# Low halves of the expert weights: all on VectorE instead of shared between VectorE and GpSimd

## The chip, the cores and the metric

One core of one Trainium2 chip runs the whole program. The metric is device time in microseconds (us), the median of three runs. Times inside the program are counted from the first profiled instruction of one profiled execution.

## The reference, cut to what matters

Three stages follow each other. Chunked attention makes 4608 token rows of 512 values. A mixture of eight experts sends each row to the expert with the largest gate logit and scales what comes back. A feed-forward part with a rational activation, P(h)/Q(h), makes the output.

```python
x = attention(q, k, v)                       # [4608, 512], chunks of 64 tokens, 8 heads
e = argmax(x @ w_gate)                       # one of 8 experts for each token
y = gate * (max(x @ w1[e], 0) @ w2[e])       # w1: [8, 512, 1024], w2: [8, 1024, 512], float32
h = y @ w_in                                 # float64 weights, [512, 2048]
out = (P(h) / (Q(h) + 1e-6)) @ w_out         # [2048, 512], float64
```

## The kernel before, in words

Every float32 matrix product of the experts and of the feed-forward part is made of three TensorE products: each operand is split into a high part (a copy rounded to the matmul type) and a low part (what the rounding left), and `mm3` (L257) adds high·high, high·low and low·high. The split of a weight tile is `split` (L132): ScalarE writes the high part (L136), and then one subtraction of a 128x1024 float32 tile writes the low part (L137). This subtraction reads two tiles in SBUF and writes a third. Its engine is the argument `eng`.

A weight tile goes through three steps. `fetch` (L208) takes one of four buffers of the pool `tmp` and has SP issue a 512 KB load. `split_w` (L139) takes a place in one of two rings of eight split tiles, and ScalarE and the engine `eng` fill it. The buffer is free for the load of the fourth tile after it once both have read it. Three callers choose the engine:

- In the attention loop, eight tiles of expert 0 are split at steps 16, 18, ... 30, all on GpSimd (L845).
- `weight()` (L228) splits the next tile of a list (`plan`) of 128 tiles for the expert stage: `w` tiles of each expert's fixed part of 512 tokens, `s` tiles for one further tile of 128 tokens, and the first half of the feed-forward weights. It is called after nearly every group of 12 products. Unless a caller names an engine, `alternate(c)` (L216) gives even tiles to VectorE and odd ones to GpSimd.
- `load_late` (L1267) splits the second half of the feed-forward weights on GpSimd, in 128x512 pieces, when the feed-forward part has begun.

What else VectorE does in the expert stage stands in the same order as in the code, because TensorE, VectorE and ScalarE keep the written order there (`manual_schedule` with MAN); GpSimd does not, and in the attention loop only TensorE keeps it, so a planner orders VectorE there. Beside the weights VectorE evacuates low parts of transposed rows (`to_T`, L255), low parts of the hidden layer (`relu`, L379) and results (L398), and in pieces rounds the float64 feed-forward weights to float32 (`convert`, L194, with `conv` at L167: L174 to L177, then L181 to L186). Most of these conversion steps read and write SBUF alone. In the attention part the chain of small operations that choose a token's expert (L681 to L690) lies on SBUF alone too. GpSimd's other work is the indirect transfers: the tokens' places (L788), gathers of rows (L237) and scatters of results (L243).

One expert of the loop `for e in range(1, NE)` takes 268 TensorE products and transposes. Within it the rows of the next expert are transposed in four steps `p(j)` into a PSUM tile of which there is only one (`ps_t`, bufs=1), so a `p(j)` has to wait until VectorE has written the low part of the one before it (L255).

Of the kernel before, what the change touches and what calls it, by code (L numbers as in the profile page):

```python
# [9 lines left out]
F32 = mybir.dt.float32  # L10
F32R = mybir.dt.float32r
BF16 = mybir.dt.bfloat16
I32 = mybir.dt.int32
U32 = mybir.dt.uint32
# [5 lines left out]
NT = 4608          # tokens  # L20
NTILE = NT // 128  # token tiles
NV = 3             # value tiles kept
NB = NT // 512     # blocks of the feed-forward part
NU = NTILE // 2    # units of two token tiles
NE = 8             # experts
BASE = 512         # slots of each expert's fixed part
LATE = 4           # the last units, whose tokens take no place among
X0 = NTILE - 2     # the step of the attention at which they do
EARLY = 384        # the first slots of expert 0: its tiles start while they are routed
NOVF = (NT - BASE) // 128   # most tiles that can lie beyond the fixed parts  # L30
NSTAT = 8          # tiles beyond the fixed parts that are unrolled
NOT_T = NT // 128  # tiles that an expert can have
PASSES = ((0, 0), (0, 1), (1, 0))   # hi*hi, hi*lo, lo*hi
CW = 256           # columns that are rounded to float32 at a time
# [3 lines left out]
EXP_BIAS = 893.0 * 2.0 ** 20   # float64's exponent bias less float32's, and 3, in place  # L38
# [3 lines left out]
def kernel(  # L42
# [19 lines left out]
    xs = dram.tile([NT, 512], F32, name="xs")               # attention's rows  # L62
    # experts' rows; behind them one row for each place that no token has
    ys = dram.tile([NT + NE * NT + NOVF * 128, 512], F32, name="ys")
    slots = dram.tile([NE * NT, 1], U32, name="slots")      # token of (expert, p, tile)
# [13 lines left out]
    # what the routing needs after the attention's end, and the other side of the SBUF  # L79
# [5 lines left out]
    # ---------------------------------------------------------------- constants  # L85
# [15 lines left out]
    rev = iota_f(once, "rev", [NE], [[-1, NE]], NE, 0)              # 8 - e  # L101
    rev2 = rev[:, None, :].to_broadcast([128, 2, NE])
    none = iota_f(once, "none", [1], [[0, 1]], NT, 1)               # row for the result of no token
# [5 lines left out]
    # the gate's weights, a quarter of the rows for each quarter of the PE array's columns,  # L109
    # and the sum of the quarters  # L110
# [7 lines left out]
    # coefficients of the rational function, P's negated  # L118
# [12 lines left out]
    # ---------------------------------------------------------------- weights  # L131
# [19 lines left out]
    # the feed-forward weights come as float64 words: rounded to float32 here  # L151
# [15 lines left out]
    def conv(job):  # L167
        raw, dst, m = job
        low, high = raw[:, :, 0], raw[:, :, 1]
        t = cv_p.tile([128, CW], I32, tag="cv", bufs=2, name=f"cv{m}")  # L170
        tf, lowf, highf = t.bitcast(F32), low.bitcast(F32), high.bitcast(F32)
        V = nc.vector
        # 2**(exponent - 3), with the sign
        V.tensor_scalar(t, high, 0x7ff00000, None, op0=ALU.bitwise_and)  # L174
        V.tensor_scalar(t, t, EXP_BIAS, EXP_BIAS, op0=ALU.max, op1=ALU.subtract)
        V.tensor_scalar(t, t, 3, None, op0=ALU.logical_shift_left)
        V.scalar_tensor_tensor(t, high, SIGN, t, op0=ALU.bitwise_and, op1=ALU.bitwise_or)  # L177

        def rest():
            # the upper 20 bits of the fraction, and the lower 32  # L180
            V.tensor_scalar(high, high, 0xfffff, 0x3f800000,  # L181
                            op0=ALU.bitwise_and, op1=ALU.bitwise_or)
            V.scalar_tensor_tensor(highf, highf, -0.875, tf, op0=ALU.add, op1=ALU.mult)
            V.scalar_tensor_tensor(lowf, low.bitcast(U32), 2.0 ** -55, tf,
                                   op0=ALU.mult, op1=ALU.mult)
            V.tensor_tensor(out=tf, in0=highf, in1=lowf, op=ALU.add)  # L186
            nc.sync.dma_start(dst, tf)

        return rest
# [4 lines left out]
    def convert(n):  # L194
        """n halves of the next jobs"""
        for _ in range(n):
            if half:
                half.pop()()
            elif fetched:
                half.append(conv(fetched.pop(0)))  # L200
            if jobs and len(fetched) + len(half) < 2:
                # behind the weights that are needed sooner
                with tc.issue_after(queued[-1]):
                    fetched.append(conv_fetch())
# [11 lines left out]
    def alternate(c):  # L216
        return nc.gpsimd if c % 2 else nc.vector

    # (source, buffers, list, place in it, name, order of the columns), in the order of use
# [14 lines left out]
    # ---------------------------------------------------------------- experts  # L234
# [14 lines left out]
    def to_T(src, hi, lo, nm, pool=None):  # L249
        # [128 rows, 512] -> four [128, 128] transposes, as hi and lo parts  # L250
        ps = (pool or ps_t).tile([128, 4, 128], F32, tag="h" if pool else "tp", name=nm)
        for c in range(4):
            nc.tensor.transpose(ps[:, c, :], src[:, 128 * c:128 * c + 128], ident)  # L253
        nc.scalar.activation(hi, ps, AF.Copy)
        nc.vector.tensor_tensor(out=lo, in0=ps, in1=hi.bitcast(F32), op=ALU.subtract)  # L255
# [50 lines left out]
    class Extra:  # L306
        """One tile of 128 tokens of any expert, in steps."""
# [51 lines left out]
    class Expert:  # L359
        """The fixed part of an expert's tokens, in steps."""  # L360
# [40 lines left out]
    # ---------------------------------------------------------------- attention  # L401
# [8 lines left out]
    # ---------------------------------------------------------------- feed-forward  # L410
# [22 lines left out]
    def first(b, c):  # L433
# [17 lines left out]
        if b == NB - 1 and c >= 12:  # L451
            # more of them at once, in the place of the next block's rows
            if c == 12:
                gts["last"] = xt_p[NB % 2].tile([128, 2, 4, 512], F32R, tag="xt", name="g_last")
            gt = gts["last"][:, :, c - 12]
        else:
            gt = h_p.tile([128, 2, 512], F32R, tag="h", name=f"g{b}_{c}")
# [26 lines left out]
    with man:  # L484
# [8 lines left out]
        for n in range(NV):  # L493
            # a pair of heads side by side: the second's columns are 0 in the first's rows,
            # the first's in the second's, so that one product takes both
            vt = v_p.tile([128, 2, 4, 2, 66], F32, name=f"v{n}")
            nc.gpsimd.memset(vt, 0.0)
            for j in range(2):
                nc.gpsimd.memset(vt[64 * j:64 * j + 64, :, :, j, 64:65], 1.0)
            vts.append(vt)  # L500
# [8 lines left out]
        def load_unit(u):  # L509
            nonlocal last_load  # L510
            r = [qk_p.tile([128, 8, 2, 64], F32, tag=nm, name=f"{nm}{u}") for nm in "qk"]
            # the first unit's in two halves, to start on the first of them
# [186 lines left out]
        # blocks' rows  # L699
        def load_rows(b):  # L700
# [6 lines left out]
            else:  # L707
                # in the place of the second block's transposed rows
# [33 lines left out]
        def early_counts():  # L742
            # what expert 0 has fewer than EARLY tokens by now
# [6 lines left out]
        def stage_rk(u):  # L750
            # ranks among the tokens of the same expert
# [14 lines left out]
            # the token's place: (expert, rank % 128, rank // 128)  # L766
# [36 lines left out]
        for i in range(NTILE + 1):  # L803
# [4 lines left out]
            if n == 0 and 0 <= g < 8:  # L808
                # expert 0's weights, behind the attention's own loads
# [33 lines left out]
            if n == 0 and 0 <= g < 8:  # L843
                with tc.issue_after(last_exp):
                    weights0[g] = split_w(raws0[g], "A", f"w0_{g}", g < 4, nc.gpsimd)  # L845
# [4 lines left out]
            # expert 0's first tiles, while the last tokens are routed  # L850
# [9 lines left out]
        # every expert's weights: of its fixed part in ring B, of its further tile in ring A  # L860
# [68 lines left out]
        # tokens of the experts' tiles  # L929
# [5 lines left out]
        # the rest of expert 0's fixed part  # L935
# [9 lines left out]
        # tiles beyond the fixed parts: (expert, tile) of the k-th one  # L945
# [59 lines left out]
        tab = const.tile([128, NOVF, 2], F32, name="tab")       # column, row if none  # L1005
        valid = small("valid", [NOVF])
        valid2 = small("valid2", [NOVF])
        etab = const.tile([128, NOVF], I32, name="etab")        # the expert
# [4 lines left out]
        pick(col, cbase)                                        # 32 e - cs  # L1013
# [15 lines left out]
        # gate probabilities  # L1029
# [10 lines left out]
        # the activation table that all that follows is in  # L1040
# [184 lines left out]
        # The first block's tokens rank below BASE among their experts' (a token's rank is at  # L1225
        # most its index), so their rows come from the fixed parts.
# [15 lines left out]
        # two products that run while the other engines come to the loop below  # L1242
# [4 lines left out]
        # the rest of the tiles beyond the fixed parts  # L1247
# [19 lines left out]
    def load_late(n):  # L1267
        # the second half's, in pieces that leave the other buffers alone
# [9 lines left out]
    # ---------------------------------------------------------------- feed-forward  # L1278
# [44 lines left out]
```

## Time and profile before

| | |
|---|---|
| three runs | 1591.93, 1591.75, 1588.03 us; median 1591.75 |
| profiled execution | span 1587.3 us; its own time beside the span is not among the times shown |
| busy in the span | TensorE 1485.4 us (94%), VectorE 1345.3 (85%), ScalarE 926.3 (58%), GpSimd 538.8 (34%) |
| GpSimd's subtractions that the change moves | 35 of `w` tiles, 87.7 us; 32 of `s` tiles, 82.5 us |
| mean granted TensorE clock | 0.974 |

The shares are means over stages with different limits. The attention part ends at about 225 us, the experts at about 745 us, and the rest is the feed-forward part. A row of a view names line, engine, operation, tiles written and read, shape and count; behind the bar stand busy time, mean ns of one instruction and the idle time before them with what ended it.

### The profile page before, as it was taken

How to read it: one execution, taken by the hardware profiler on the slowest of the kernel's cores; microseconds unless marked ns; L12 is line 12 of the kernel's file. 1: busy time of each engine (PE TensorE's matmuls, PEld its weight loads, DVE VectorE, ACT ScalarE, POOL GpSimd, SP SyncE). 2: the span in 40 equal slices, each digit the busy share in tenths (PEclk: the TensorE clock that was granted, in tenths of full speed). 3: DMA queues.
4: the chain of work that ended last, by engine and by line, in shares of the span. 5: the costliest groups of instructions: out<-in, count | busy, mean ns of one | idle time of the engine just before them, and what ended most of it. 6: DMA issues, size and time to landing. Idle time of an engine off the chain costs nothing.

```text
span 1587.3 us, 22356 instructions
## 1 busy us (share of the span) xinstructions
PE 1485.4 (94%) x7812; PEld 1213.4 (76%) x7812; DVE 1345.3 (85%) x2338; ACT 926.3 (58%) x1456; POOL 538.8 (34%) x374
## 2 busy tenths in 40 slices
PE   6888899998988989899889999999999999999998
PEld 5777777786867768677667888888888888888886
DVE  6788867799999999997788889888888888888886
ACT  5676644443434344344667666667676767676765
POOL 2123334544536355352453232322222222222222
PEclk9999999999989899999999999999999999999999
DMA  8999625676666676665220001010000101000000
GB/s 186 225 256 231 179 80 180 216 243 229 211 208 227 215 248 205 222 209 196 93 68 20 34 1 47 1 40 14 27 27 14 40 1 43 11 34 1 27 1 27
DMA packets 143377, 180.07 MB, mean 113 GB/s; under 512 B 51616, under 2 KB 96672, under 8 KB 143264
## 3 DMA queue, kind: packets, MB, share of 16 engines
q1 hardware_dynamic: 135712, 157.64, 33.0%
q0 software_dynamic: 7552, 21.00, 4.0%
q8 instruction: 62, 1.02, 0.3%
q14 instruction: 51, 0.42, 0.1%
HBM read 140.68 MB, written 37.91 MB: 113 GB/s over the span
## 4 chain that ended last, share of the span: by engine, by line
PE 45%; DVE 2%; issue 2%; POOL 1%; ACT 1%; DMA 0%; SPq 0%; ACTq 0%; POOLq 0%
PE z L259 23%; PE f L259 22%; PE ytp L253 1%; POOL g L459 1%; DVE t L449 1%; POOL wf L137 1%; DVE t L448 0%; DVE t L450 0%; DVE t L444 0%; DMA yg<-ys 0%; DVE t L446 0%; ACT u L445 0%; ACT t L440 0%; ACT t L441 0%; ACT u L442 0%
## 5 line engine op out<-in xcount | busy, mean ns | idle before, releaser
L259 PE MATMUL f<-yT,wf 128*128 128x512 f32 x1728 | 421.1, 395 | 5.7 <-DVE t L446 2.2
L259 PE MATMUL z<-wf,g 128*128 128x512 f32 x1680 | 411.1, 395 | 6.8 <-POOL g L459 4.1
L459 POOL TENSOR_TENSOR g<-t,g 128x512 fp32r<-128x512 f32 x140 | 209.5, 1498 | 531.8 <-ACT g L458 497.4
L259 PEld LDWEIGHTS f<-yT,wf 128*128 128x128 f32 x1728 | 324.7, 189 | 81.0 <-DVE t L446 3.1
L259 PEld LDWEIGHTS z<-wf,g 128*128 128x128 f32 x1680 | 314.7, 189 | 80.0 <-POOL g L459 5.9
L259 PE MATMUL y<-w,hT 128*128 128x512 f32 x744 | 195.7, 413 | 1.5 <-DVE hT L379 1.3
L443 DVE TENSOR_TENSOR t<-t,f 128x512 f32<-128x512 f32 x144 | 98.5, 684 | 100.7 <-ACT u L442 100.4
L259 PE MATMUL h<-xT,w 128*128 128x512 f32 (+1 forms) x768 | 182.0, 386 | 0.0
L259 PEld LDWEIGHTS y<-w,hT 128*128 128x128 f32 x744 | 144.6, 199 | 33.6 <-DVE hT L379 2.4
L259 PEld LDWEIGHTS h<-xT,w 128*128 128x128 f32 x768 | 142.3, 188 | 28.9 <-DVE hT L379 1.4
L444 DVE SCALAR_TENSOR_TENSOR t<-t,co,u 128x512 f32<-128x512 f32 x144 | 159.0, 1104 | 0.0
L445 ACT ACTIVATE u<-t,cq 128x512 f32<-128x512 f32 x144 | 104.6, 726 | 85.2 <-DVE t L444 84.7
L458 ACT ACTIVATE g<-t 128x512 fp32r<-128x512 f32 x140 | 89.0, 636 | 99.4 <-DVE t L450 99.3
L440 ACT ACTIVATE t<-f,co 128x512 f32<-128x512 f32 x144 | 112.0, 778 | 50.2 <-PE f L259 34.9
L137 POOL TENSOR_TENSOR w<-raw_w,w 128x1024 fp32r<-128x1024 f32 x35 | 87.7, 2506 | 120.9 <-ACT w L136 90.1
L450 DVE SCALAR_TENSOR_TENSOR t<-t,co 128x512 f32<-128x512 f32 x144 | 122.0, 847 | 2.0
L136 ACT ACTIVATE s<-raw_s 128x1024 fp32r<-128x1024 f32 x64 | 69.9, 1097 | 81.5 <-DMA raw_s<-in_moe_w_dram 81.5
L448 DVE SCALAR_TENSOR_TENSOR t<-t,u 128x512 f32<-128x512 f32 x144 | 101.7, 706 | 15.5 <-ACT u L447 15.5
L137 POOL TENSOR_TENSOR s<-raw_s,s 128x1024 fp32r<-128x1024 f32 x32 | 82.5, 2577 | 80.9 <-ACT s L136 80.7
L449 DVE SCALAR_TENSOR_TENSOR t<-t,u 128x512 f32<-128x512 f32 x144 | 109.5, 760 | 0.5
L442 ACT ACTIVATE u<-f,co 128x512 f32<-128x512 f32 x144 | 98.2, 682 | 15.0 <-DVE t L449 10.9
L446 DVE SCALAR_TENSOR_TENSOR t<-t,co,f 128x512 f32<-128x512 f32 x144 | 106.1, 737 | 0.0
(205 smaller groups left out, 2153.3 us busy)
## 6 DMA issues: line engine op xcount, KB each, us to landing
raw_w<-in_moe_w_dram SPq DMA_DIRECT2D x64, 512.0 KB
raw_s<-in_moe_w_dram SPq DMA_DIRECT2D x64, 512.0 KB
v<-in_v_dram SPq DMA_DIRECT2D x144, 64.0 KB
xs<-x SPq DMA_DIRECT2D x36, 256.0 KB
out_dram<-o SPq DMA_DIRECT2D x36, 256.0 KB
raw<-in_moe_w_in_dram SPq DMA_DIRECT2D x32, 256.0 KB
raw<-in_moe_w_out_dram SPq DMA_DIRECT2D x32, 256.0 KB
yg<-ys SPq DMA_DIRECT2D x32, 256.0 KB
```

The costliest lines, as they stand in the source:

```text
L137: eng.tensor_tensor(out=lo, in0=raw, in1=hi.bitcast(F32), op=ALU.subtract)
L259: nc.tensor.matmul(o, lhsT=lhs(x), rhs=rhs(y), start=(first and n == 0), stop=(last and n == 2))
L440: nc.scalar.activation(p, hp, AF.Identity, scale=a3, bias=a2)
L442: nc.scalar.activation(vv, hp, AF.Abs, scale=b0)
L443: V.tensor_tensor(out=p, in0=p, in1=hp, op=ALU.mult)
L444: V.scalar_tensor_tensor(qq, qq, b1, vv, op0=ALU.mult, op1=ALU.add)
L445: nc.scalar.activation(r, qq, AF.Abs_reciprocal_sqrt, bias=cq)
L446: V.scalar_tensor_tensor(p, p, a1, hp, op0=ALU.add, op1=ALU.mult)
L448: V.scalar_tensor_tensor(qq, qq, CQ, r, op0=ALU.add, op1=ALU.mult)
L449: V.scalar_tensor_tensor(qq, qq, -2.0, r, op0=ALU.add, op1=ALU.mult)
L450: V.scalar_tensor_tensor(p, p, a0, qq, op0=ALU.add, op1=ALU.mult)
L459: nc.gpsimd.tensor_tensor(out=gt[:, 1], in0=p, in1=gt[:, 0].bitcast(F32), op=ALU.subtract)
```

## The change

`alternate` returns VectorE for every tile, and the eight tiles of expert 0 that are split in the attention loop are given to VectorE. `load_late` keeps GpSimd. `load_extra`, which also calls `alternate`, is used in a loop that no tile of these inputs enters. Comments are taken out as well, with the line numbers kept.

```diff
     def alternate(c):
-        return nc.gpsimd if c % 2 else nc.vector
+        return nc.vector
...
             if n == 0 and 0 <= g < 8:
                 with tc.issue_after(last_exp):
-                    weights0[g] = split_w(raws0[g], "A", f"w0_{g}", g < 4, nc.gpsimd)
+                    weights0[g] = split_w(raws0[g], "A", f"w0_{g}", g < 4, nc.vector)
```

## Rows read from the trace of the kernel before

**Rows 1.** Page, part 2: VectorE's busy tenths and the granted TensorE clock, 40 slices.
```profile
DVE  6788867799999999997788889888888888888886
...
PEclk9999999999989899999999999999999999999999
```
**Rows 2.** Windows: stretch, length, busy us by engine, granted clock, DMA share, GB/s.
```profile
96.00:160.00 64.00, 51.82 (x603) 44.71 (x603) 54.17 (x168) 43.08 (x70) 23.57 (x17) 0.95 0.96 241
225.00:290.00 65.00, 61.53 (x316) 51.17 (x315) 41.25 (x91) 29.26 (x43) 29.46 (x20) 1.00 0.51 166
443.00:510.80 67.80, 61.28 (x269) 49.78 (x268) 64.92 (x110) 27.58 (x36) 31.47 (x18) 0.92 0.67 219
```
**Rows 3.** Waits, 290 to 745 us: total us, times, longest us.
```profile
ACT s L136 <- DMA raw_s<-in_moe_w_dram: 81.5, 31, 4.6
...
PE xtp L253 <- DVE xT L255: 35.9, 6, 6.9
```
**Rows 4.** Windows at TensorE's idle time, and behind it (sum of five such stretches).
```profile
443.00:449.90 6.90, 0.38 (x3) 0.03 (x1) 6.66 (x16) 2.18 (x3) 1.00 (x1) 0.69 0.84 286
...
382.20:387.60 5.40, 5.02 (x14) 4.15 (x15) 5.23 (x8) 2.90 (x4) 3.73 (x2) 0.51 0.97 367
...
sum 24.50, PE 23.84 PEld 19.69 DVE 22.03 ACT 12.90 POOL 16.17; mean PE 4.77 PEld 3.94 DVE 4.41 ACT 2.58 POOL 3.23
```
**Rows 5.** Timeline, VectorE and GpSimd, 490 to 496 us: start us, length us, instruction.
```profile
490.44 5.32 DVE L181 TENSOR_SCALAR raw<-raw 128x256 int32<-128x256 int32 x1
...
490.80 2.41 POOL L137 TENSOR_TENSOR w<-raw_w,w 128x1024 fp32r<-128x1024 f32 x1
...
493.15 2.45 POOL L137 TENSOR_TENSOR s<-raw_s,s 128x1024 fp32r<-128x1024 f32 x1
```
**Rows 6.** Single lines of the kernel: ns shortest/median/longest, first and last start.
```profile
L181 DVE TENSOR_SCALAR raw<-raw x64: 286/295/5344, 295.5 to 723.7; 128x256 int32<-128x256 int32 x64
...
L174 DVE TENSOR_SCALAR cv<-raw x64: 279/286/2536, 294.0 to 720.1; 128x256 int32<-128x256 int32 x64
```
**Rows 7.** Groups of VectorE's instructions, 290 to 745 us, by form.
```profile
L181 DVE TENSOR_SCALAR raw<-raw 128x256 int32<-128x256 int32 x64 | 65.3, 1020 | 1.3
L174 DVE TENSOR_SCALAR cv<-raw 128x256 int32<-128x256 int32 x64 | 45.6, 713 | 1.8 <-DMA raw<-in_moe_w_out_dram 1.8
...
L137 DVE TENSOR_TENSOR w<-raw_w,w 128x1024 fp32r<-128x1024 f32 x24 | 29.2, 1218 | 0.4 <-ACT w L136 0.2
...
L175 DVE TENSOR_SCALAR cv<-cv 128x256 int32<-128x256 int32 x64 | 27.6, 431 | 2.2
...
L176 DVE TENSOR_SCALAR cv<-cv 128x256 int32<-128x256 int32 x64 | 26.2, 409 | 2.2
```
**Rows 8.** Groups of GpSimd's instructions, 290 to 745 us.
```profile
L137 POOL TENSOR_TENSOR s<-raw_s,s 128x1024 fp32r<-128x1024 f32 x29 | 75.1, 2588 | 78.2 <-ACT s L136 78.0
L137 POOL TENSOR_TENSOR w<-raw_w,w 128x1024 fp32r<-128x1024 f32 x24 | 61.3, 2554 | 110.9 <-ACT w L136 81.3 <-DMA raw<-in_moe_w_out_dram 29.5
```
**Rows 9.** Waits, 96 to 233 us.
```profile
PE qkp L569 <- DVE kT L576: 17.5, 8, 2.7
```
**Rows 10.** Timeline, one unit of the attention loop, 122 to 128 us.
```profile
122.52 1.14 ACT L136 ACTIVATE w<-raw_w 128x1024 fp32r<-128x1024 f32 x1
...
123.74 2.40 POOL L137 TENSOR_TENSOR w<-raw_w,w 128x1024 fp32r<-128x1024 f32 x1 [0.66 <-ACT w L136]
...
123.89 2.29 DVE L684 TENSOR_TENSOR e<-lg_all,mx_all 128x16 f32<-128x16 f32 x1
...
126.83 0.69 DVE L576 COPY kT<-qkp 64x512 f32<-64x512 f32 x1
...
127.58 1.49 PE L569 MATMUL qkp<-ident,qkr 128*128 128x128 f32 x8 [2.71 <-DVE kT L576]
```
**Rows 11.** Groups of VectorE's instructions, 40 to 96 us.
```profile
L684 DVE TENSOR_TENSOR e<-lg_all,mx_all 128x16 f32<-128x16 f32 x6 | 1.0, 165 | 0.0
```
**Rows 12.** Timeline: load, high part and low part of one tile, 502 to 514 us.
```profile
502.14 1.22 DVE L137 TENSOR_TENSOR s<-raw_s,s 128x1024 fp32r<-128x1024 f32 x1
...
503.38 0.34 SPq L210 DMA_DIRECT2D raw_s<-in_moe_w_dram  x1
...
507.17 1.06 ACT L136 ACTIVATE s<-raw_s 128x1024 fp32r<-128x1024 f32 x1 [2.28 <-DMA raw_s<-in_moe_w_dram]
...
512.62 1.22 DVE L137 TENSOR_TENSOR s<-raw_s,s 128x1024 fp32r<-128x1024 f32 x1
```

## The prediction

> **What bounds the kernel now.** I read the page's slices first. VectorE is busy nine tenths or more from slice 9 to slice 18, which is the expert stage, and the granted clock of TensorE dips in the same part [rows 1]. The windows then separate the stages. One expert of the steady loop takes 67.8 us: VectorE is busy 64.9 of them, TensorE 61.3, at a mean clock of 0.92 [rows 2]. Between 225 and 290 us it is the other way, TensorE 61.5 of 65 and VectorE 41.3 [rows 2].
>
> The waits say how VectorE bounds the experts: TensorE waits there in one place, for the low part of a transposed tile from VectorE, 35.9 us in 6 waits, the longest 6.9 [rows 3]. That is one wait for each expert. In the window of such a wait VectorE is busy 6.66 of 6.9 us and TensorE 0.4; behind it TensorE works at a granted clock of about 0.5, the lower of its two levels (1.2 instead of 2.4 GHz), and five such stretches sum to 24.5 us [rows 4]. So VectorE is late, and TensorE pays for that twice.
>
> Why is VectorE late? The timeline shows one conversion step (L181) of 5.32 us. Two of GpSimd's subtractions, 2.41 and 2.45 us, lie inside it, one behind the other [rows 5]. The median of that instruction is 295 ns [rows 6]. An operation of VectorE on SBUF alone that comes while GpSimd subtracts ends only when GpSimd does. The instruction 5.32 us long is mostly a wait that the view counts as busy.
>
> **The change part by part.** 67 subtractions leave GpSimd: 8 in the attention loop, 53 (29 and 24) between 290 and 745 us [rows 8], and 6 between.
>
> *What VectorE gains in the expert stage.* I compare the mean with the median for the two conversion steps with both: L181 (1020 - 295) x 64 = 46.4 us, L174 (713 - 286) x 64 = 27.3 us. L175 and L176 are the same operation and shape; with 295 for each they lose (431 - 295) x 64 = 8.7 and (409 - 295) x 64 = 7.3 us [rows 6, 7]. That is 89.7 us, or 1.69 us for each of the 53 subtractions, a lower end because smaller groups are left out. The upper end is the pair seen directly, (5.32 - 0.30) / 2 = 2.5 us [rows 5]. I take 1.95, a little nearer the lower end, which sums over all instructions of these lines.
>
> *What VectorE pays.* Its own subtraction of such a tile takes 1218 ns [rows 7], against 2.55 to 2.59 us on GpSimd [rows 8]. Net VectorE gains 1.95 - 1.22 = 0.73 us for each moved tile. An expert has 8 of them, so 5.8 us (between 3.8 and 10).
>
> *What of it is on the path.* Of the six waits, the five large ones are about 6.7 us each. If VectorE comes 5.8 us earlier, 0.9 us stays in each: 35.9 - 5 x 0.9 = 31.4 us go. The 24.5 us at the lower clock held half the work, so 12.2 us come back if the clock no longer falls behind a wait this short. Together 43.6 us. The bounds: if all idle time goes it is 35.9 + 12.2 = 48.1; if VectorE sheds only 3.8 us, each wait stays near 2.9 us, which may be enough for the clock to fall, and 5 x 3.8 = 19 us are gained. What is late next is TensorE itself: 67.8 - 6.5 of idle - 2.4 of clock (a fifth of 12.2) leaves about 58.9 us of its own work for an expert, against 64.9 - 15.6 + 9.7 = 59.0 for VectorE. The two nearly meet, so I leave a rest of waiting.
>
> *The attention loop.* Eight times TensorE waits for VectorE's copy of k (L576), 17.5 us in total [rows 9]. The timeline of one unit shows why: GpSimd subtracts from 123.74 for 2.40 us; VectorE's tiny L684, begun at 123.89, takes 2.29 us; the copy of k comes at 126.83, and TensorE has idled 2.71 us [rows 10]. Undisturbed, L684 takes 165 ns [rows 11]. So 2.1 us are lost for each tile, and 1.22 takes their place if the subtraction stands ahead of the copy: 8 x 0.9 = 7 us gained, my value. If the planner puts it where VectorE has time, all 17.5 go, and some 6 us of lower clock that follow these waits by the windows' mean of 0.95 [rows 2]. If VectorE instead waits in line for ScalarE's high part (1.14 us [rows 10]), it is 8 x (1.22 + 1.14 - 2.1) = 2 us slower.
>
> *The six tiles between.* Between 225 and 290 us TensorE is the bound and VectorE has 24 us free [rows 2]; 6 x 1.22 = 7.3 us fit. I count nothing; without that cover it is 7.3 us.
>
> *Waits that are added.* VectorE now stands in line for the high part of every tile, and relu, transposed rows and conversions queue behind it, TensorE behind those. In the sample the load was issued at 503.38, the high part began at 507.17, and VectorE came to it only at 512.62, 4.4 us after the high part was written [rows 12]. That lead covers the wait. GpSimd's gathers and scatters no longer queue behind subtractions; nothing on TensorE's path waits for them, so nothing is counted. SP issues a load when its buffer is free, and only VectorE's progress releases it now: no new queue. The feed-forward part keeps its work.
>
> The Trainium skill, Perfetto Trace Analysis, section Optimizing Scalar/DVE Operations, speaks against the change: if DVE is saturated, some work may be given to ScalarE or even GpSimd. By that alone the moved work would come on top of the engine that bounds the experts. The same section adds that both share a read port, so that moving work between these two may not help. The conversion step of 5.32 us under two subtractions [rows 5] agrees with the addition.
>
> The sum: 43.6 + 7 = 50.6 us. Against the profiled span it is 1587.3 - 50.6 = 1536.7. The runs lie 0.7 to 4.6 us above that span (1588.03 to 1591.93), so the median becomes 1591.75 - 50.6, **about 1541 us**.
>
> **Rivals.**
>
> *More than that.* The attention's waits go as a whole. For it: units before 96 us have no such wait, and L684 is short there [rows 11]. Against it: DMA's share is 0.96 from 96 to 160 us [rows 2], so the loads would hold the loop soon. 43.6 + 17.5 + 6 = 67 us, 1525 us.
>
> *Half of it.* The stalls are at their lower end, the clock still falls and the attention gains nothing: 19 to 22 us, 1570 us. For it: VectorE and TensorE come within 1 us of each other in an expert, so each wait of VectorE for ScalarE counts.
>
> *Slower: VectorE waits for late tiles.* ScalarE waits 81.5 us for loads of `s` tiles, 31 times [rows 3]. All odd tiles of these were off VectorE's line. It decides when VectorE's work between one tile and the fourth after it becomes shorter than load, high part and low part: 3.8 + 1.06 + 1.22 = 6.1 us, against 512.62 - 503.36 = 9.3 us now [rows 12]. If all 81.5 us came on VectorE's path, 81.5 - 50.6 = 31 us would be lost: 1623 us. Against it: the 9.3 us hold two stalls (4 us less) and gain two subtractions (2.4 more), which leaves 7.7.
>
> *Slower: the stalls have another cause* and stay. Then VectorE has 67 x 1.22 = 82 us more where it is the bound: 1674 us. Against it stand the ends of instructions on both engines [rows 5, 10]. The rule of the Trainium skill's Perfetto Trace Analysis (Optimizing Scalar/DVE Operations) on a saturated VectorE would by itself give this time.
>
> **How the numbers follow.** Forecast 0.70, more 0.12, half 0.13, late tiles 0.03, other cause 0.02. The range: from 1520 (48.1 + 17.5 + 6 = 72 us gained) to 1570, the half case. About 0.3% is what a measurement of this kernel can tell from no change, 5 us. Faster holds the first two cases and most of the third, 0.92; same is what the half case leaves when late tiles eat the rest, 0.03; slower the last two, 0.05.
>
> **What would show it.** In the profile after: medians and means of L181, L174 and L684 nearly equal; no GpSimd subtraction before 745 us; TensorE's wait for L255 under 6 us in total and the clock at 1.00 through the experts; an expert's period near 59 to 60 us; the waits for L576 at about 10 us in total. It is wrong if VectorE's idle time before L137 grows to several us per expert, if the period stays above 64 us, or if the conversion steps stay long without GpSimd's subtractions.

## The result, and the profile after

The kernel after takes 1547.87 us (median of 4 runs, 1544.71 to 1549.44) against 1591.84 us before: a ratio of 0.9723, 95% interval 0.9705 to 0.9740, or 44 us. The forecast was 1541 us in a range of 1520 to 1570. The profiled execution took 1549.44 us with a span of 1547.7, 39.6 us shorter than the span before.

Where the 39.6 us lie can be read from two lines of the code. The last L684, near the end of the attention loop, starts at 229.7 us (229.1 before), and the first L440, at the start of the feed-forward part, at 717.7 (757.8 before). Between them 40.7 us are gone; the attention loop gave nothing here. (One profile cannot tell a few us in that loop: in another execution of the same kernel, E9 below, it ends at 221.0 us. The stretch between the two lines is 488.7 us there and 488.0 here.) The stretch as a whole, before and after (columns as in [rows 2]):

```profile
229.10:757.80 528.70, 484.68 (x2175) 393.57 (x2173) 475.75 (x810) 221.97 (x294) 234.89 (x139) 0.96 0.65 212
```

```profile
229.70:717.70 488.00, 474.41 (x2175) 385.92 (x2174) 420.23 (x869) 222.68 (x295) 91.87 (x80) 0.99 0.71 230
```

TensorE's idle time fell by 30.4 us, and its busy time for the same products by 10.3 us, at a higher clock. The page after (part 2, the rows that answer to [rows 1], and GpSimd's):

```profile
DVE  6787857799889898985989888888888888888886
...
POOL 2111122121211212102542222222222222222232
PEclk9999999999999999999999999999999999999999
```

In tenths TensorE's clock shows no dip in the experts' slices any more (two short ones are left, in the windows below), and VectorE is no longer full through all of them. The groups of VectorE, 290 to 710 us, answer to [rows 7]; the last two numbers ahead of the second bar are busy us and mean ns:

```profile
L137 DVE TENSOR_TENSOR w<-raw_w,w 128x1024 fp32r<-128x1024 f32 x48 | 58.5, 1219 | 0.0
...
L176 DVE TENSOR_SCALAR cv<-cv 128x256 int32<-128x256 int32 x64 | 19.6, 307 | 2.2
L175 DVE TENSOR_SCALAR cv<-cv 128x256 int32<-128x256 int32 x64 | 19.2, 300 | 2.2
L181 DVE TENSOR_SCALAR raw<-raw 128x256 int32<-128x256 int32 x64 | 18.5, 289 | 0.3
L174 DVE TENSOR_SCALAR cv<-raw 128x256 int32<-128x256 int32 x64 | 18.3, 286 | 0.0
```

The same 256 instructions shed 64 x (1020 - 289 + 713 - 286 + 431 - 300 + 409 - 307) ns = 89 us, and nothing in them was changed but GpSimd's company. VectorE's own subtraction of a `w` tile costs the 1219 ns that it cost before. The windows of three experts (columns as in [rows 2]):

```profile
407.00:469.10 62.10, 60.24 (x269) 48.72 (x269) 56.13 (x119) 27.25 (x37) 11.80 (x11) 0.97 0.74 242
469.10:530.30 61.20, 60.24 (x268) 48.73 (x268) 56.03 (x119) 26.32 (x36) 11.63 (x11) 0.97 0.76 244
530.30:592.50 62.20, 59.00 (x269) 47.49 (x269) 56.30 (x119) 28.60 (x38) 12.59 (x11) 1.00 0.78 241
```

An expert takes 62 us instead of 67.8, and VectorE is busy 56 us of them instead of 64.9. TensorE is busy 95 to 98 parts of a hundred: it is the bound now. What is left is in the waits, 290 to 710 us (to be set beside [rows 3]):

```profile
DVE yo L398 <- DMA ys<-yo,sidx: 17.0, 5, 4.1
ACT s L136 <- DMA raw_s<-in_moe_w_dram: 16.3, 20, 2.0
...
PE h L259 <- DVE hT L379: 6.4, 4, 1.8
...
PE xtp L253 <- DVE xT L255: 4.1, 6, 1.2
```

The wait for L255 fell from 35.9 us to 4.1. In its place stands a new one: VectorE waits up to 4.1 us for a scatter, and TensorE behind it up to 1.8 us. The timeline shows its place:

```profile
396.06 1.20 POOL L243 DMA_INDIRECT ys<-yo,sidx  x1 [0.30 <-issue]
...
397.86 0.98 POOL L243 DMA_INDIRECT ys<-yo,sidx  x1 [0.60 <-DVE cv L174]
...
403.10 0.69 DVE L398 COPY yo<-y 128x512 f32<-128x512 f32 x1 [4.12 <-DMA ys<-yo,sidx]
...
406.30 0.69 DVE L379 SCALAR_TENSOR_TENSOR hT<-h,hT 128x512 fp32r<-128x512 f32 x1
...
407.04 4.55 PE L259 MATMUL h<-xT,w 128*128 128x512 f32 x12 [1.83 <-DVE hT L379]
```

There are two buffers for output tiles (`o_p`). VectorE copies output tile 2 of the expert before into a buffer whose scatter was issued only a few us ago. By the semaphores of the trace it is the scatter issued at 396.06, of the tile that ScalarE had copied; it has landed at 403.00, and VectorE stood ready at 398.98. The low part L379 is queued behind that copy, and TensorE behind L379. In the kernel before VectorE came later, and the scatter had just landed:

```profile
478.49 1.06 POOL L243 DMA_INDIRECT ys<-yo,sidx  x1 [0.30 <-ACT yo L396]
...
483.96 0.69 DVE L398 COPY yo<-y 128x512 f32<-128x512 f32 x1 [0.55 <-ACT hTs L254]
```

There VectorE stood ready 4.9 us after the issue and the landing took 5.3 us; after, it is 2.9 and 6.9 us. Why the transfer takes longer is not shown.

### The profile page after: what moved, and what is told of

Read it like the earlier page. It is cut to its first block, busy times and chain, and to the rows that moved or that the text cites. A ratio compares the mean times of both kernels' runs of the same rounds, so it can differ in the third digit from the quotient of the medians.

```text
span 1547.7 us, 22303 instructions
## 1 busy us (share of the span) xinstructions
PE 1471.6 (95%) x7812; PEld 1198.5 (77%) x7812; DVE 1284.8 (83%) x2405; ACT 927.2 (60%) x1456; POOL 376.8 (24%) x307
## 4 chain that ended last, share of the span: by engine, by line
PE 46%; DVE 3%; issue 2%; POOL 1%; ACT 1%; DMA 0%; SPq 0%; ACTq 0%; POOLq 0%
PE z L259 23%; PE f L259 23%; PE ytp L253 1%; POOL g L459 1%; DVE t L449 1%; POOL wf L137 1%; DVE t L448 0%; DVE t L444 0%; DVE t L450 0%; DMA yg<-ys 0%; DVE t L446 0%; ACT u L445 0%; ACT t L440 0%; DVE yg L718 0%; DVE t L443 0%
## 5 line engine op out<-in xcount | busy, mean ns | idle before, releaser
L259 PE MATMUL y<-w,hT 128*128 128x512 f32 x744 | 184.0, 396 | 0.0
L259 PEld LDWEIGHTS y<-w,hT 128*128 128x128 f32 x744 | 136.9, 188 | 28.2 <-issue 0.4
L440 ACT ACTIVATE t<-f,co 128x512 f32<-128x512 f32 x144 | 112.1, 778 | 49.4 <-PE f L259 34.2
L378 ACT ACTIVATE hT<-h 128x512 fp32r<-128x512 f32 (+1 forms) x64 | 37.5, 585 | 147.0 <-PE h L259 114.1
L442 ACT ACTIVATE u<-f,co 128x512 f32<-128x512 f32 x144 | 98.3, 683 | 15.0 <-DVE t L449 10.9
L447 ACT ACTIVATE u<-u 128x512 f32<-128x512 f32 x144 | 90.4, 628 | 2.2
L441 ACT ACTIVATE t<-f 128x512 f32<-128x512 f32 x144 | 85.1, 591 | 0.0
```

The costliest lines, as they stand in the source:

```text
L259: nc.tensor.matmul(o, lhsT=lhs(x), rhs=rhs(y), start=(first and n == 0), stop=(last and n == 2))
L440: nc.scalar.activation(p, hp, AF.Identity, scale=a3, bias=a2)
L442: nc.scalar.activation(vv, hp, AF.Abs, scale=b0)
L447: last_act = nc.scalar.activation(r, r, AF.Square).ins
```

## The experiments

Ratios are to the kernel before, with 95% intervals. E1 to E4 were measured on one chip, E5 to E8 on a second, E9 to E12 on a third, each group beside the kernel before.

**E1: the attention loop alone.**

```diff
 # kernel before
-weights0[g] = split_w(raws0[g], "A", f"w0_{g}", g < 4, nc.gpsimd)
+weights0[g] = split_w(raws0[g], "A", f"w0_{g}", g < 4, nc.vector)
```

> The kernel before, with the eight tiles of the attention loop alone moved to VectorE. Theory of the prediction: 8 x (2.1 - 1.22) = 7 us faster than before, about 1585 us. Rival A: the loop gains nothing whoever subtracts (in the profile of the kernel after, its units take 11.8 to 11.9 us, as before), because the high part on ScalarE or the loads hold the loop: 1592 us, within 2 us of before. Units of 11.9 us either way would bear out the rival.

Measured: 1589.61 us, ratio 1.0025 (1.0008 to 1.0042). The seven microseconds of the prediction are not there; the kernel is even 4 us slower by the median. Where it loses them is not shown: in E1's profile the loop ends at 222.0 us, earlier than in the kernel before, and loop ends scatter by more than this. TensorE's waits, 96 to 233 us, of the kernel after show what became of the 17.5 us of [rows 9]:

```profile
PE xtp L652 <- DVE x L642: 5.1, 4, 1.8
PE xtp L652 <- ACT qkr L550: 4.7, 4, 1.2
...
PE ru_all L671 <- ACT lt L665: 4.2, 1, 4.2
...
PE qkp L569 <- ACT xt L656: 4.0, 8, 1.2
...
PE qkp L569 <- issue: 2.8, 6, 0.6
```

The wait for the copy of k has gone, and five smaller ones sum to 20.8 us. L684 has no stall left in this kernel (median 167 ns, longest 176), so the stall itself did go.

**E2: the experts alone.** The kernel after, with that one line back on GpSimd.

```diff
 # kernel after
-weights0[g] = split_w(raws0[g], "A", f"w0_{g}", g < 4, nc.vector)
+weights0[g] = split_w(raws0[g], "A", f"w0_{g}", g < 4, nc.gpsimd)
```

> The kernel after, with the eight tiles of the attention loop given back to GpSimd. If the whole gain comes from the 59 later tiles: 1548 us, within 3 us of the kernel after. If the attention loop gave 7 us of the 44: 1555 us.

Measured: ratio 0.9719 (0.9684 to 0.9753), against 0.9723 for the whole change. The other 59 tiles bring all of the gain.

**E3: half of the odd tiles back on GpSimd.**

```diff
 # kernel after
     def alternate(c):
-        return nc.vector
+        return nc.gpsimd if c % 4 == 3 else nc.vector
```

> The kernel after, with every fourth tile (the last of each four, half of the 59) back on GpSimd. Theory: each GpSimd subtraction stalls VectorE by about 2 us, so the conversion steps keep about half of their excess (the mean of L181 near 600 to 700 ns, between 289 and 1020) and the time is about half way: 1560 to 1575 us. Rival (VectorE has spare time now and takes any mix): within 3 us of 1548. Rival (two engines share the work best): below 1545 us.

Measured: 1589.93 us, ratio 1.0026 (1.0008 to 1.0044). Half of the moved work undone takes away all of the gain, which no theory had expected. The mean of L181 was forecast at 600 to 700 ns and is 395: the stalls fell on other instructions as well. E3's timeline shows why; lines of both engines:

```profile
425.83 6.23 DVE L137 TENSOR_TENSOR s<-raw_s,s 128x1024 fp32r<-128x1024 f32 x1
...
426.19 2.40 POOL L137 TENSOR_TENSOR w<-raw_w,w 128x1024 fp32r<-128x1024 f32 x1
...
428.54 2.43 POOL L137 TENSOR_TENSOR s<-raw_s,s 128x1024 fp32r<-128x1024 f32 x1
...
442.45 2.43 DVE L181 TENSOR_SCALAR raw<-raw 128x256 int32<-128x256 int32 x1
...
447.39 1.12 PE L253 MATMUL xtp<-ident,xg 128*128 128x128 f32 x4 [8.07 <-DVE xT L255]
```

A subtraction on VectorE of 1.2 us takes 6.23, because two of GpSimd's run back to back inside it. The Trainium skill, SBUF — State Buffer, section Who interferes with whom, says that a VectorE instruction with two SBUF inputs contends with a GpSimd instruction that reads SBUF, and that the issue order decides who blocks. The rows agree on the contention, and they add that VectorE did not get in between two GpSimd instructions in a row. On the order they do not decide: by the records the VectorE instruction began first (425.83 against 426.19), and it is the one that waited. A further stall of 2.1 us follows at 442 us. Together 7.2 us lie in the last 22 us before TensorE's wait for the transposed rows ends (447.39), and that wait is 8.07 us long, longer than any in the kernel before [rows 3]. In the same stretch VectorE also waits 1.75 us for a load of float64 weights (11.2 us in 5 such waits from 290 to 745 us; the kernel after has none), so the stalls are not the whole of it. The waits of E3 in sum, 290 to 745 us:

```profile
PE xtp L253 <- DVE xT L255: 42.8, 6, 8.6
DVE yo L398 <- DMA ys<-yo,sidx: 18.1, 6, 4.0
```

What VectorE saves earlier in the expert it loses in the wait for the scatter. So not the sum of the stalls but their place seemed to count. E10 tests that.

**E4: every tile of the list on GpSimd that no caller gives to VectorE.**

```diff
 # kernel after
     def alternate(c):
-        return nc.vector
+        return nc.gpsimd
```

> All tiles of the expert list on GpSimd that the callers do not pin to VectorE (even ones too); attention tiles on VectorE. VectorE then does 8 subtractions fewer per expert than in the kernel before (9.8 us less of its own work) and 16 fewer than after. Theory of the stall: 16 GpSimd subtractions an expert, each stalling VectorE by about 2 us: 64.9 - 9.8 + 8 x 1.95 = 70.7 us an expert against 67.8, so slower than before by 15 to 40 us, 1607 to 1632. Rival (the long conversion steps have another cause, and VectorE's own work sets the pace): VectorE sheds 59 us over the stage and the kernel is as fast as after or faster, 1545 to 1550. GpSimd itself has room: 16 x 2.55 + 10 = 51 us of an expert.

Measured: 1688.42 us, ratio 1.0645 (1.0591 to 1.0699). VectorE has less work of its own than in any other kernel here, and the time is the longest: the rival that sees only VectorE's own work is out. The direction is the theory's, the size is not (102 us against 15 to 40). Groups and waits, 290 to 745 us:

```profile
L181 DVE TENSOR_SCALAR raw<-raw 128x256 int32<-128x256 int32 x55 | 59.7, 1085 | 1.3
L176 DVE TENSOR_SCALAR cv<-cv 128x256 int32<-128x256 int32 x55 | 55.8, 1015 | 1.9
```

```profile
ACT s L136 <- DMA raw_s<-in_moe_w_dram: 113.8, 26, 12.1
...
PE xtp L253 <- DVE xT L255: 60.7, 10, 7.5
PE h L259 <- DVE hT L379: 29.9, 8, 9.6
...
DVE cv L174 <- DMA raw<-in_moe_w_out_dram: 19.5, 9, 3.6
DVE cv L174 <- DMA raw<-in_moe_w_in_dram: 17.1, 10, 3.4
```

There are more stalls, TensorE waits in two places, and ScalarE and VectorE wait longer for loads. That these start late because buffers come free late is argued from the code. From the last L684 to the first L440 (221.3 to 855.3 us) VectorE is busy 527.0 us against 475.8 before, 51 us more; the theory's 5.8 us for each of eight experts make 46. The stretch grew by 105 us, so about half of the loss is time in which VectorE waits, and that half the theory did not have. No wait of TensorE for GpSimd's own low parts is listed.

**E5 and E11: the copy of output tile 2 later.**

```diff
 # kernel after, in the loop over experts
                 cur.first(0)
-                old.out(2)
                 weight()
                 convert(1)
                 cur.relu(0)
                 late.t(1)
+                old.out(2)
                 cur.first(1)
```

> The kernel after, with the copy of output tile 2 of the expert before put behind the hidden layer's low part and one transposed tile, instead of ahead of them. In the kernel after VectorE waits 4.1 us there for the scatter of an earlier output tile (17.0 us, 5 times), and TensorE then waits 1.8 us for the low part (6.4 us in all) and runs 3.4 us at the lower clock twice. Theory (this is the wait that took the place of the old one): the wait for the low part goes, 6.4 + 3.4 = 10 us faster than after, about 1537 us, an expert near 59 us instead of 62. Rival (the wait for the scatter only moves, and VectorE is late for the next thing): within 3 us of after.

Measured: ratio 0.9692 (0.9671 to 0.9713). Its waits, 290 to 710 us:

```profile
DVE w L137 <- ACT w L136: 11.2, 7, 4.1
...
PE xtp L253 <- DVE xT L255: 8.0, 9, 3.2
...
DVE yo L398 <- DMA ys<-yo,sidx: 0.6, 2, 0.4
```

The wait for the scatter is gone (17.0 to 0.6 us), and no wait of TensorE for L379 is listed any more; 8.0 us at L255 remain. The gain is a few us, so it was measured again beside the kernel after on one chip, as E11 with E9:

> The kernel with the copy of output tile 2 later, once more beside after on one chip: 3 to 9 us faster than after (the stage of the experts was 5 us shorter in the profile).

> The kernel after once more, on the same chip as the next three, as their common measure: 0.972 of before, 1545 to 1551 us where before runs at 1592.

Measured on one chip: kernel after (E9) 1545.15 us, 0.9743 (0.9725 to 0.9762); copy later (E11) 1537.85 us, 0.9699 (0.9680 to 0.9717). It is 7 us faster (10 were forecast for E5), and the new wait is shown to have cost about that. An expert of E11 takes 60 us:

```profile
484.20:544.10 59.90, 58.67 (x268) 47.58 (x268) 56.44 (x119) 27.82 (x36) 11.80 (x10) 1.00 0.78 248
```

**E6, E7, E8: what holds the attention loop.** Each was timed once, so only the length of the loop's units is read. A unit is the time from one L684 to the next, here the mean of five units between about 125 and 186 us.

```diff
 # E6, kernel after: the high part stands in for the low part of expert 0
-weights0[g] = split_w(raws0[g], "A", f"w0_{g}", g < 4, nc.vector)
+nc.scalar.activation(hi, raw, AF.Copy)
+weights0[g] = w[:, 0:1].to_broadcast([128, 2, 1024])
 # E7, kernel after: one load, split eight times
-raws0[g] = fetch((w1r if g < 4 else w2r)[0, g % 4], f"w0_{g}")
+raws0[g] = raws0[0] if g else fetch(w1r[0, 0], "w0_0")
 # E8, kernel after: one tile, loaded and split once, in the place of all eight
+weights0[g] = weights0[0] or split_w(raws0[0], "A", "w0_0", True, nc.vector)
```

> The kernel after, without the eight subtractions of expert 0 in the attention loop: the products take the high part in the low part's place, so expert 0's low parts are left out. Loads and high parts stay. If the subtraction is what holds the loop's units at 11.8 us, they fall to 9.5 to 10.5 us and the loop ends 8 to 18 us sooner; if the high part on ScalarE or the loads hold them, they stay at 11.5 us or more.

> The kernel after, with one load for expert 0: all eight tiles are split from the same 512 KB, so seven loads (3.6 MB) are left out, and high and low parts are written eight times as after. If the loads hold the loop (DMA share 0.91 to 0.96 from 40 to 160 us), the units fall below 11 us; if not, they stay at 11.8 us and the DMA share falls.

> The kernel after, with one tile for all eight of expert 0: seven loads, high parts and subtractions are left out of the attention loop. If the tiles are what lengthens the units from about 9.5 us (before 96 us) to 11.8, they stay near 9.5 us, and the loop ends some 15 us sooner. If they stay at 11 us or more, the loop is held by its own chain of operations, and neither engine's subtraction could have gained there.

Measured: E6 11.1 us, E7 11.9, E8 9.4, against 11.9 in the kernel after and 12.2 before. But E1, whose engines have the same order in this loop as in the kernel after, has 11.2, and E2, with the order of before, 11.5. E10 has 12.1 with the order of after, E12 10.9 with the order of before. So two executions of the same loop differ by up to 1.3 us, and E6 cannot be told from a kernel with the subtraction. Loads are not it: DMA's share from 96 to 160 us fell from 0.91 to 0.80 in E7 and the units stayed. The tiles as a whole are it: without seven of them (E8) the units, 9.4 us, lie below that spread, and the loop ends at 216.1 us, ahead of every other kernel. Ends of the loop (last start of L684) in E1 and E8:

```profile
L684 DVE TENSOR_TENSOR e<-lg_all,mx_all x18: 164/165/176, 40.6 to 222.0; 128x16 f32<-128x16 f32 x18
```

```profile
L684 DVE TENSOR_TENSOR e<-lg_all,mx_all x18: 165/166/176, 40.8 to 216.1; 128x16 f32<-128x16 f32 x18
```

What remains beside the subtraction is the high part on ScalarE, 1.1 us in each unit. It was not taken out alone, so whether it or the subtraction holds the loop stays open.

**E10: 14 tiles on GpSimd, early in each expert.** The kernel after, with one constant more, so its lines stand one further down.

```diff
+ODD = {f"w1_{e}_{c}" for e in range(1, 8) for c in (1, 3)}
...
-                        eng or alternate(c if type(c) is int else c[1]))
+                        nc.gpsimd if nm in ODD else nc.vector)
```

> The kernel after, with 14 tiles back on GpSimd: the second and fourth w1 tile of each expert from 1 to 7, which are split early in an expert, ahead of the place where VectorE then waits 4.1 us for the scatter of an output tile. Theory after the run with half of the odd tiles: it is not the sum of the stalls that counts but where they lie, and only those between that wait and TensorE's wait for the transposed rows (some 40 us later) are paid. Then these 14 cost nothing: within 4 us of after in the same call. Rival (the sum of the stalls counts): 14 x (2.1 - 1.22) = 12 us slower than after.

Measured: 1542.39 us, 0.9730 (0.9707 to 0.9753), against 0.9743 for the kernel after on the same chip: no loss. The stalls are there (timeline of both engines):

```profile
391.02 3.01 POOL L138 TENSOR_TENSOR w<-raw_w,w 128x1024 fp32r<-128x1024 f32 x1 [3.20 <-ACT w L137]
...
391.65 2.53 DVE L175 TENSOR_SCALAR cv<-raw 128x256 int32<-128x256 int32 x1
```

But they fall into time that VectorE would have waited. First the waits of E9, the kernel after on the same chip, then those of E10, both 290 to 710 us:

```profile
DVE yo L398 <- DMA ys<-yo,sidx: 19.9, 6, 4.2
...
PE h L259 <- DVE hT L379: 7.0, 4, 1.9
```

```profile
PE xtp L254 <- DVE xT L256: 9.4, 10, 2.3
...
DVE yo L399 <- DMA ys<-yo,sidx: 0.8, 3, 0.4
```

VectorE's 19.9 us of waiting for the scatter are 0.8 here. 14 GpSimd subtractions in one place cost nothing, half of the odd ones (29) spread over the list (E3) cost all 44 us. The counts differ, so this alone would not tell place from sum. VectorE's busy time (third column of engines) from the last L684 to the first L440 does, in E9, E10 and E3:

```profile
221.00:709.70 488.70, 473.15 (x2176) 384.70 (x2174) 420.40 (x870) 222.98 (x295) 93.52 (x80) 1.00 0.72 229
```

```profile
226.10:710.90 484.80, 470.91 (x2175) 383.47 (x2173) 433.71 (x855) 222.72 (x295) 122.40 (x94) 1.00 0.72 231
```

```profile
224.70:762.60 537.90, 481.64 (x2176) 392.53 (x2174) 452.53 (x840) 221.37 (x295) 159.71 (x109) 0.96 0.65 208
```

E10 is busy 13.3 us more than E9 and no slower. E3 is busy 23.2 us less than the kernel before (475.75) and no faster, while 18.1 us of VectorE's waiting for the scatter stay unused. That is the place, not the sum. A run with as many tiles late in each expert was not made.

**E12: copy later, attention loop on GpSimd.** E5 with E2's line.

> The copy later and the eight tiles of the attention loop on GpSimd as in the kernel before. If where those eight are split is worth nothing: within 4 us of the kernel with the copy later. If the loop with VectorE is the slower one (the run of the attention part alone was 1.0025 of before): 2 to 6 us faster, the best of all.

Measured: 1535.91 us, 0.9683 (0.9664 to 0.9703). It is within 2 us of E11, whose interval it overlaps, and 9 us faster than the kernel after: the best version here beats both kernels.

## Why the prediction was right, point by point

- *VectorE bounds the experts, blocked by GpSimd.* Right. The four lines of the conversion are short again, E4 lengthens them and the time, and VectorE's own work cannot explain either.
- *1.95 us stall for a tile, 1.22 us paid.* Somewhat too low. The four lines alone shed 89 us, the lower end of 1.69 us by 53. With all lines VectorE's busy time fell by 55.5 us (475.75 to 420.23) for 59 tiles, 0.94 us net for each where 0.73 was forecast; for an expert by 8.8 us (64.9 to 56.1), where 5.8 was forecast within 3.8 to 10.
- *Which part of it is on the path.* Right for this change, but not as a rule. I priced every stall of an expert alike. E3 and E10 show that a stall is paid only where VectorE has no wait behind it that takes it up before TensorE waits. In the kernel before VectorE hardly waited (busy 64.9 of 67.8 us, and no wait of it for a scatter is listed), so nearly every stall was paid.
- *0.9 us of waiting left in each expert.* The wait for L255 is 4.1 us in 6, forecast 4.5; that is luck, because with 8.8 us shed the same subtraction (6.7 - 8.8) leaves none. The wait that came instead was put at nothing: of gathers and scatters the prediction says that nothing on TensorE's path waits for them. VectorE did wait for the scatter, through the two output buffers, and TensorE behind it. That costs 6.4 us of TensorE's time and two dips of the clock, and is why an expert takes 62 us and not 59 to 60. E11, without that wait, takes 60 us for an expert and gets 7 us back.
- *12.2 us of clock.* Most came back: TensorE's busy time fell by 10.3 us, and the clock is 0.97 and 1.00 in the windows above against 0.92.
- *Late tiles on VectorE's line.* The rival did not come: ScalarE's waits for `s` loads fell from 81.5 to 16.3 us. That loads start earlier when buffers come free earlier is argued, not shown.
- *7 us in the attention loop.* Wrong, and the mis-sized term of the sum: 8 x (2.1 - 1.22) measured -4 us in E1. The stall went, as said, and the waits for L576, put at about 10 us, went wholly; but the gap of TensorE was taken for the price of the stall, and other waits of about the same sum took its place. What holds the loop instead stays open.
- *The sum.* 43.6 + 7 forecast, 40.7 - 0.6 in the profiled executions, 44 by the medians. Of the 43.6, 31.4 us of TensorE's idle time and 12.2 us of clock were forecast; 30.4 and 10.3 were measured. That the idle time comes so near is in part luck: VectorE shed more than forecast, and the new wait took some of it back.

## What to carry to other kernels

Before work is given to GpSimd to relieve VectorE, look for VectorE instructions whose longest duration is many times their median, and whether GpSimd's instructions end where they do: a busy VectorE may be a blocked one. Where such work has to stay on GpSimd, put it where VectorE is about to wait anyway, never in the last stretch before the wait of the bounding engine. And when an engine that was late comes early, ask which buffer's transfer its lateness has hidden.

## What the runs showed of the hardware that was not expected

VectorE stayed blocked across two GpSimd subtractions in a row, 5.32 us for a step of 0.29 [rows 5] and 6.23 us for one of 1.22 (E3). Both VectorE instructions began about 0.36 us ahead of the first of the two subtractions by the records, so the record's start does not tell which engine gets in first. TensorE's granted clock fell behind a wait of 1.83 us (0.97 in the window from 407.0), but not behind one of 1.84 us in E9 (1.00 from 399.0 to 461.0 us): waits of one length did and did not cost clock.
